# Theta as one product over all 512 columns, a new order of its stage, and two row blocks in each float64 piece

## The chip, the cores and the metric

One core of one Trainium2 chip runs the whole program in one launch. The metric is device time in microseconds of that core. Three runs of the kernel before took 546.91, 547.48 and 551.65 us; their median is 547.48 us.

## The reference

Four batches, 576 tokens. What is computed, in order, all in float32 except where the input is float64:

```python
# 1. attention, 8 heads of 64; heads 0-3 local (32 keys back), 4-7 strided (same position mod 32)
attn = softmax(where(mask, q @ k.T / 8, -1e9)) @ v          # -> x, 4 x 576 x 512
# 2. mixing; its weights arrive as float64
theta = x @ w_theta
y = w_tok_r @ (x * cos(theta)) + w_tok_i @ (x * sin(theta))
u = x + y
x = u + relu(u @ w_ch)
# 3. four experts, two of four taken per token, each a causal attention of 64
out = sum_e gate_e * (softmax(causal(x wq_e (x wk_e).T / 8)) @ (x wv_e) @ wo_e)
```

## The kernel before

Every float32 product that must keep its precision is made of three products of rounded halves (`mm3`, lines 291 to 294): hi by hi, hi by lo, lo by hi. So each operand is split by a copy (hi) and a subtraction (lo).

The **attention** of a batch is worked in four pairs of heads (`attn_pair`), pairs 0 and 1 local, 2 and 3 strided, each in three groups. Its result for batch b goes to the tile `X[b]`, features on the partitions. The attention of batch 0 comes first. That of batch b+1 (`next_pair`) is written between the steps of the mixing of batch b, so that TensorE has something to do in both.

The **mixing** of a batch has five steps. `theta(b, h)` makes, for one half h of the features (256 columns) and five blocks of tokens t (four of 128, one of 64), 12 products of 256 columns, rounds theta/2pi on VectorE (lines 315, 316), and takes the absolute value (line 317), the cosine (line 329) and the sine (line 330) on ScalarE. `rotate(b, h)` transposes x on TensorE into `xn`, multiplies it with cosine and sine (line 348; 354 and 355 for the last block) and splits the result into `z` (lines 358 or 360, and 362). `tokens(b, h)` makes four accumulations `y` of 27 products of 288 columns over the nine row blocks of the token weights `wtk`, adds x (line 377) and splits the sum `u` (lines 386, 387). `channels(b)` makes eight accumulations `g` of 12 products with the weights `wch` and adds them (line 399); it comes one batch later, behind `theta(b+1, 0)`.

The order written out for a batch b over 0 is theta(b,0), pair 0 of b+1, channels(b-1), rotate(b,0), pair 1, theta(b,1), pair 2, rotate(b,1), tokens(b,0), pair 3, tokens(b,1). On ScalarE, sines and exponentials need different tables, and `issue_after` keeps them together: in batches over 0 the ten sines and cosines of a half come behind the last absolute value of that half, and exponentials of pairs 1 and 3 come behind the sines of the half.

The **float64 weights** (`load64`, lines 139 to 145) come by DMA on SyncE's queue, one row block of 128 rows to a piece, into slots of `X[1]` and `X[3]`, four in each. A piece costs one copy on ScalarE (143), one bit operation on VectorE (144), and the split: one activation on ScalarE (106), one subtraction on VectorE (108 or 110). w_theta has 8 pieces of 256 columns, w_tok 18 of 288 in two halves of nine, w_ch 8 of 256.

Buffers that the change touches: `act` (four of the tags ahi and alo) holds the split of x for theta; `zu` (four) holds z of half 0 and then the split u; `z1` holds z of half 1; `rp` (five) holds cosine and sine; in PSUM, `acc` (two banks) holds th, y and g, `s` scores, and in batch 0 also th of odd blocks.

What stands in the program is the wanted order; a planner simulates the engines when the kernel is built and moves instructions of an engine past each other where buffers and `issue_after` allow. The order that runs is its order.

Of the kernel before, what the change touches and what calls it, by code (L numbers as in the profile page):

```python
# [48 lines left out]
def fused_kernel(ctx: ExitStack, tc: tile.TileContext, ql, kl, vl, qs, ks, vs, q0l, q0s, wth, wtk, wch, wqk, wvg, wo, out):  # L49
# [25 lines left out]
    mask_l = new_mask("mask_l", [128, 4, LK], wb)  # L75
# [4 lines left out]
    nc.vector.tensor_copy(mask_l[:64, 2:4, :], mask_l[:64, 1:2, :].to_broadcast([64, 2, LK]))  # L80
# [45 lines left out]
    def load64(dst, src, kt, n0, n1, scale=1.0, late=False):  # L126

        hi, lo = dst
        n = n1 - n0
        for c in range(kt):
            place = X[3] if late or len(pieces) % 2 else X[1]
            raw = place.bitcast(U16)[:, len(pieces) // (1 if late else 2) % 4, :4 * n]
            pieces.append(c)
            st = X[2][:, c % 4, HALF:HALF + n]
            nc.sync.dma_start(raw[:, :4 * n - 1], src[:, c, n0:n1].bitcast(U16)[:, 1:])
            mid = raw.bitcast(U32).rearrange("p (n t) -> p n t", t=2)[:, :, 0]  # L140
# [45 lines left out]
    def attn_pair(b, pair, ps1, apl, deep):  # L186
# [6 lines left out]
        for g, (j0, j1) in enumerate(groups):  # L193
# [4 lines left out]
            mask = mask_l[:, min(g, 1):min(g, 1) + 3, :] if local else mask_s[:, 2 * (g // 2):2 * (g // 2) + n, :]  # L198
# [103 lines left out]
    def theta(b, h):  # L302
        if h == 0:
            xsplit[b] = split_x(b)
        xs = xsplit[b]
        d0 = 256 * h
        for t in range(NT):
            w, t0 = TW[t], 128 * t
            th = ps1.tile([128, 512], F32, tag="s" if b == 0 and t % 2 else "acc", bufs=2, name=f"th_{b}_{h}_{t}")
            for c in range(4):  # L310
                turned = mm3(th[:w, :256], xs[c][0][:, t0:t0 + w], xs[c][1][:, t0:t0 + w],
                             wth_hi[:, c, d0:d0 + 256], wth_lo[:, c, d0:d0 + 256], c == 0, c == 3)
            cs = rp.tile([128, 2, 256], F32, tag="cs", name=f"cs_{b}_{h}_{t}")
            r = cs[:w, 1, :]
            nc.vector.tensor_scalar_add(r, th[:w, :256], MAGIC)
            nc.vector.scalar_tensor_tensor(r, r, MAGIC, th[:w, :256], op0=ALU.subtract, op1=ALU.subtract)  # L316
            last = nc.scalar.activation(cs[:w, 0, :], r, AF.Abs)
            trig[h, t] = cs
            if b == 0:
                sines(b, h, range(t, t + 1))  # L320
# [5 lines left out]
    def sines(b, h, tiles):  # L326
        for t in tiles:
            w, cs = TW[t], trig[h, t]
            nc.scalar.activation(cs[:w, 0, :], cs[:w, 0, :], AF.Sin, bias=halfpi[:w], scale=-TWO_PI)
            sins[b, h] = nc.scalar.activation(cs[:w, 1, :], cs[:w, 1, :], AF.Sin, scale=-TWO_PI).ins  # L330

    def rotate(b, h):
        for t in range(NT):
            w, t0, cs = TW[t], 128 * t, trig[h, t]
# [4 lines left out]
            if t < 4:  # L339
                zf = cs  # L340
                if h == 0:
                    hi = zu.tile([128, S], F32R, tag="zuhi", name=f"zhi_{b}_{h}_{t}")
                    lo = zu.tile([128, S], F32R, tag="zulo", name=f"zlo_{b}_{h}_{t}")
                else:
                    hi = z1.tile([128, 512], F32R, tag=f"zhi{t}", name=f"zhi_{b}_{h}_{t}")
                    lo = z1.tile([128, 512], F32R, tag=f"zlo{t}", name=f"zlo_{b}_{h}_{t}")
                hi, lo = (v[:, :512].rearrange("p (a c) -> p a c", a=2) for v in (hi, lo))
                nc.vector.tensor_tensor(zf, cs, xn[:, None, :256].to_broadcast([128, 2, 256]), op=ALU.mult)
                z[h, t], z[h, 4 + t] = (hi[:, 0, :], lo[:, 0, :]), (hi[:, 1, :], lo[:, 1, :])
            else:  # L350
# [51 lines left out]
    nc.gpsimd.memset(halfpi, math.pi / 2)  # L402
    spark = const.tile([128, 1], F32, name="spark")
# [5 lines left out]
    with tc.tile_pool(name="ps0", bufs=2, space=PSUM) as ps0, tc.tile_pool(name="ain0", bufs=9) as ain0, \  # L409
# [445 lines left out]
```

## Time and profile before

| | |
|---|---|
| median of three runs | 547.48 us |
| the profiled execution | 551.44 us, span 549.6 us |
| TensorE (PE) busy | 524.4 us, 95% |
| VectorE (DVE) busy | 402.3 us, 73% |
| ScalarE (ACT) busy | 319.7 us, 58% |
| GpSimd (POOL) busy | 195.4 us, 36% |
| chain that ended last | PE 72%, DVE 12%, ACT 6%, DMA 6% |

Times count from the start of the span. A busy PE is one that has a product in flight; since products overlap, two that follow each other show their true cost by the distance of their starts. The attention of batch 0 lasts to about 36 us, the mixing with the attention of the other batches to about 346 us, the experts to the end.

### The profile page before, as it was taken

What the parts mean: (1) busy time and instruction counts of PE and PEld (TensorE: products, weight loads), DVE (VectorE), ACT (ScalarE), POOL (GpSimd) and SP (SyncE); (2) the same over time, 40 slices, a digit from 0 to 9 for tenths busy, and PEclk for the clock granted to TensorE, in tenths of its full rate; (3) what the DMA queues carried; (4) which work ended last, traced back from release to release, by engine and by line L of the source; (5) the groups of instructions that cost most, each with busy time, mean ns of one, the idle gap of its engine ahead of it and who ended that gap; (6) DMA issues with size and microseconds to landing.
All of it is one profiled execution on the core that took longest, in us unless ns stands there. A gap on an engine that the chain in (4) does not pass through costs nothing.

```text
span 549.6 us, 12463 instructions
## 1 busy us (share of the span) xinstructions
PE 524.4 (95%) x4500; PEld 499.9 (91%) x4500; DVE 402.3 (73%) x1269; ACT 319.7 (58%) x906; POOL 195.4 (36%) x280
## 2 busy tenths in 40 slices
PE   6798999989999999999999999999999999999997
PEld 5688899989999999989999999979988998999987
DVE  5979996765857576855456443699998888888972
ACT  4988984426362163352145431487788767867873
POOL 5100013320643112642006462175456443625541
PEclk9959999989999999999999999999999999999999
DMA  9967243550202131000100021000001001100112
GB/s 263 282 189 257 82 162 99 172 180 24 68 23 90 35 131 35 24 23 2 58 0 1 2 60 38 1 2 1 1 16 61 14 1 45 44 1 10 36 45 87
DMA packets 20389, 36.63 MB, mean 67 GB/s; under 512 B 2904, under 2 KB 12296, under 8 KB 20328
## 3 DMA queue, kind: packets, MB, share of 16 engines
q1 hardware_dynamic: 20328, 35.83, 20.4%
q8 instruction: 36, 0.59, 0.5%
q14 instruction: 25, 0.20, 0.1%
HBM read 31.10 MB, written 4.72 MB: 65 GB/s over the span
## 4 chain that ended last, share of the span: by engine, by line
PE 72%; DVE 12%; ACT 6%; DMA 6%; issue 2%; POOL 1%; SPq 0%; DVEq 0%; ACTq 0%; POOLq 0%
PE y L292 6%; PE y L293 6%; PE y L294 6%; PE av L269 4%; PE s L205 3%; PE g L292 3%; PE g L294 3%; PE g L293 3%; PE tp L674 3%; PE tp L241 3%; PE th L294 3%; PE th L292 3%; PE th L293 2%; PE pq L292 2%; PE s L633 2%
## 5 line engine op out<-in xcount | busy, mean ns | idle before, releaser
L292 PE MATMUL y<-wtk_hi,zhi 128*128 128x288 f32 x288 | 86.0, 300 | 1.5 <-DVE cs L316 1.1
L293 PE MATMUL y<-wtk_lo,zhi 128*128 128x288 f32 x288 | 85.4, 298 | 0.0
L294 PE MATMUL y<-wtk_hi,zlo 128*128 128x288 f32 x288 | 85.2, 297 | 0.0
L238 POOL TENSOR_TENSOR p<-p,sm 128x288 f32<-128x288 f32 (+2 forms) x36 | 21.9, 615 | 136.8 <-DMA X<-in_wch 58.1
L669 POOL TENSOR_SCALAR p<-p,sm,gt 128x256 f32<-128x256 f32 (+3 forms) x63 | 45.1, 717 | 53.3 <-DVE sm L667 24.9
L292 PEld LDWEIGHTS y<-wtk_hi,zhi 128*128 128x128 f32 x288 | 53.9, 188 | 1.9 <-ACT wtk_hi L106 1.2
L293 PEld LDWEIGHTS y<-wtk_lo,zhi 128*128 128x128 f32 x288 | 54.1, 188 | 0.1
L294 PEld LDWEIGHTS y<-wtk_hi,zlo 128*128 128x128 f32 x288 | 54.0, 188 | 0.0
L362 POOL TENSOR_TENSOR zlo<-cs,zhi 128x512 fp32r<-128x512 f32 (+1 forms) x30 | 36.0, 1214 | 49.0 <-DVE zhi L358 41.3
L292 PE MATMUL th<-wth_hi,x_hi 128*128 128x256 f32 (+1 forms) x160 | 47.6, 299 | 0.9 <-ACT X L276 0.5
L293 PE MATMUL th<-wth_lo,x_hi 128*128 128x256 f32 (+1 forms) x160 | 45.5, 286 | 0.0
L294 PE MATMUL th<-wth_hi,x_lo 128*128 128x256 f32 (+1 forms) x160 | 45.2, 288 | 0.0
L205 PE MATMUL s<-k,q 128*108 128x54 f32 (+2 forms) x320 | 41.3, 270 | 1.1 <-POOL q L175 1.1
L288 POOL TENSOR_TENSOR x_lo<-X,x_hi 128x576 fp32r<-128x576 f32 x20 | 29.4, 1469 | 36.2 <-DVE x_hi L286 30.5
L245 ACT COPY pt<-tp 96x384 f32<-96x384 f32 (+2 forms) x44 | 21.1, 479 | 36.3 <-PE tp L241 35.8
L205 PEld LDWEIGHTS s<-k,q 128*108 128x108 f32 (+1 forms) x320 | 39.4, 192 | 2.0 <-POOL q L175 1.4
L292 PE MATMUL pq<-x_hi,wqk_hi 128*128 128x288 f32 x128 | 39.6, 310 | 1.3 <-DVE q L581 1.1
L292 PE MATMUL g<-u_hi,wch_hi 128*128 128x288 f32 x128 | 38.7, 302 | 0.0
L683 DVE TENSOR_TENSOR ptlo<-tp,pthi 128x128 fp32r<-128x128 f32 (+4 forms) x80 | 37.6, 479 | 1.1 <-ACT pthi L682 0.4
L293 PE MATMUL pq<-x_lo,wqk_hi 128*128 128x288 f32 x128 | 37.9, 296 | 0.0
L293 PE MATMUL g<-u_lo,wch_hi 128*128 128x288 f32 x128 | 37.8, 295 | 0.0
L294 PE MATMUL pq<-x_hi,wqk_lo 128*128 128x288 f32 x128 | 37.8, 295 | 0.0
(183 smaller groups left out, 1713.9 us busy)
## 6 DMA issues: line engine op xcount, KB each, us to landing
X<-in_wtk SPq DMA_DIRECT2D x18, 287.8 KB
q<-in_ql SPq DMA_DIRECT2D x7, 576.0 KB
q<-in_qs SPq DMA_DIRECT2D x6, 594.0 KB
v<-in_vl SPq DMA_DIRECT2D x24, 144.0 KB
out_t<-X SPq DMA_DIRECT2D x20, 128.0 KB
k<-in_kl SPq DMA_DIRECT2D x8, 304.0 KB
k<-in_ks SPq DMA_DIRECT2D x8, 288.0 KB
X<-in_wth SPq DMA_DIRECT2D x8, 255.8 KB
```

The costliest lines, as they stand in the source:

```text
L205: nc.tensor.matmul(s[:rm, i * kw:i * kw + w], qt[:, j0 + i, :], kt[:, k0:k0 + w], start=False, stop=i == n - 1)
L238: (nc.vector if b == 0 else nc.gpsimd).tensor_tensor(tiles(p), tiles(p), each(sm), op=ALU.mult)
L241: turned = nc.tensor.transpose(tp[:kw, i * rm:(i + 1) * rm], p[:rm, i * kw:(i + 1) * kw], ident[:rm, :rm])
L245: copy(pt[:kw, :n * rm], tp[:kw, :n * rm])
L269: last = nc.tensor.matmul(av[64 * h:64 * h + 64, c0:c0 + wi], vg[:w, i, h, :], pt[:w, i, h, :wi], start=True, stop=True)
L288: halved[name] = eng.tensor_tensor(lo, x, f(hi), op=ALU.subtract).ins
L292: nc.tensor.matmul(ps, ahi, bhi, start=first, stop=False)
L293: nc.tensor.matmul(ps, ahi, blo, start=False, stop=False)
L294: return nc.tensor.matmul(ps, alo, bhi, start=False, stop=last)
L362: halved[b, h] = eng.tensor_tensor(lo, zf, f(hi), op=ALU.subtract).ins
L669: eng.tensor_scalar(p[:w, :kn], p[:w, :kn], sm[:w, t:t + 1], gt[:w, t, e:e + 1], op0=ALU.mult, op1=ALU.mult)
L683: nc.vector.tensor_tensor(dst(ptlo), src, f(dst(pthi)), op=ALU.subtract)
```

## The change

Theta is made over both halves at once, in products of 512 columns, and one block of tokens at a time: `theta(b, t)`. Rounding, absolute value, cosine and sine work on 512 columns. For the last block of 64 tokens, cosine and sine share one tile of 128 partitions (absolute value in the upper half, with its own bias), so that one activation makes both. In batch 0, the first half of `wtk` is loaded two row blocks at a time between the blocks of theta, and rotate(0,0) runs one block behind; in the others both rotations come behind the whole of theta. z takes buffers of `act` for one half and of `zu` (now six) for the other; `z1` is gone. A float64 piece holds two row blocks where there are two: 4, 10 and 4 pieces, in two slots of double size for each of `X[1]`, `X[3]` and the scratch `X[2]`.

```diff
     def load64(dst, src, kt, n0, n1, scale=1.0, late=False):
-        for c in range(kt):
+        for c in range(*kt, 2):
+            m = min(2, kt[1] - c)
-            raw = place.bitcast(U16)[:, len(pieces) // (1 if late else 2) % 4, :4 * n]
+            i0 = 2 * (len(pieces) // (1 if late else 2) % 2)
+            raw = place.bitcast(U16)[:, i0:i0 + m, :4 * n]
+            j0 = 2 * (len(pieces) % 2)
-            st = X[2][:, c % 4, HALF:HALF + n]
+            st = X[2][:, j0:j0 + m, HALF:HALF + n]
...
-                with tc.issue_after(sins[b - 1, pair // 2]) if (b > 1 and pair % 2) else nullcontext():
+                with tc.issue_after(sins[b - 1]) if (b > 1 and pair == 1) else nullcontext():
...
+    def theta(b, t):
+        w, t0 = TW[t], 128 * t
+        th = ps1.tile([128, DM], F32, tag="s" if b == 0 and t % 2 else "acc", bufs=2, name=f"th_{b}_{t}")
+        for c in range(4):
+            turned = mm3(th[:w], xs[c][0][:, t0:t0 + w], xs[c][1][:, t0:t0 + w], wth_hi[:, c, :], wth_lo[:, c, :],
+                         c == 0, c == 3)
+        if t < 4:
+            cs = rp.tile([128, 2, DM], F32, tag="cs", name=f"cs_{b}_{t}")
+            first = turn = cs[:, 1, :]
+            size = cs[:, 0, :]
+        else:
+            cs = rp.tile([128, DM], F32, tag="cs4", bufs=1, name=f"cs_{b}_{t}")
+            first, turn, size = cs[0:64], cs[64:128], cs[0:64]
...
+        if b == 0:
+            sines(b, range(t, t + 1))
+        elif t == NT - 1:
             with tc.issue_after(last.ins):
-                sines(b, h, range(NT))
+                sines(b, range(NT))
...
+                sins[b] = nc.scalar.activation(cs, cs, AF.Sin, bias=quarter, scale=-TWO_PI).ins
...
     def rotate
+                pool, tags = (act, ("ahi", "alo")) if (b == 0) == (h == 1) else (zu, ("zuhi", "zulo"))
...
-    zu = ph1.enter_context(tc.tile_pool(name="zu", bufs=4))
-    rp = ph1.enter_context(tc.tile_pool(name="rp", bufs=5))
-    z1 = ph1.enter_context(tc.tile_pool(name="z1", bufs=1))
+    zu = ph1.enter_context(tc.tile_pool(name="zu", bufs=6))
+    rp = ph1.enter_context(tc.tile_pool(name="rp", bufs=4))
...
     for b in range(B):
-        theta(b, 0)
+        for t in range(NT):
+            turned = theta(b, t)
+            if b == 0:
+                with tc.issue_after(valued[0]), tc.issue_after(halved["x0_0_3"]):
+                    load64(wtk_s, wtk, (2 * t, min(2 * t + 2, 9)), 0, HALF)
+                if t > 0:
+                    rotate(b, 0, [t - 1])
         if b > 0:
             next_pair(b, 0)
             channels(b - 1)
+            rotate(b, 0)
+            next_pair(b, 1)
+            next_pair(b, 2)
         else:
-            with tc.issue_after(valued[0]), tc.issue_after(halved["x0_0_3"]):
-                load64(wtk_s, wtk, 9, 0, HALF)
-        rotate(b, 0)
-        if b > 0:
-            next_pair(b, 1)
-        turned = theta(b, 1)
-        if b > 0:
-            next_pair(b, 2)
+            rotate(b, 0, [NT - 1])
         rotate(b, 1)
...
         if b == 0:
-            with tc.issue_after(turned), tc.issue_after(sins[0, 1]):
+            with tc.issue_after(turned), tc.issue_after(sins[0]):
                 next_pair(b, 0)
                 next_pair(b, 1)
```

## Rows read from the trace of the kernel before

**Rows 1.** By stretch: us; PE, PEld, DVE, ACT, POOL busy (instructions); granted clock; DMA.

```profile
26.00:36.00 10.00, 9.31 (x107) 7.02 (x105) 7.19 (x22) 7.75 (x25) 0.00 (x0) 0.50 0.43 137
36.00:50.00 14.00, 13.65 (x101) 13.42 (x102) 13.05 (x33) 11.83 (x30) 0.00 (x0) 0.88 0.99 339
50.00:58.00 8.00, 5.42 (x44) 4.77 (x43) 7.86 (x20) 7.25 (x20) 0.00 (x0) 1.00 0.10 26
58.00:80.00 22.00, 21.14 (x163) 20.70 (x164) 21.94 (x60) 20.15 (x60) 1.93 (x2) 1.00 0.46 150
98.50:122.00 23.50, 21.57 (x287) 19.95 (x286) 17.78 (x54) 8.44 (x25) 8.25 (x10) 0.93 0.51 165
122.00:190.00 68.00, 67.94 (x638) 66.80 (x634) 42.60 (x109) 28.90 (x63) 22.71 (x23) 1.00 0.18 58
```

**Rows 2.** PE by time: start, us, line, operation, count, idle before and releaser.

```profile
54.34 0.41 PE L338 MATMUL xn<-ident,X 128*128 128x128 f32 x2 [1.66 <-DVE cs L355]
58.16 0.37 PE L292 MATMUL y<-wtk_hi,zhi 128*128 128x288 f32 x1 [1.08 <-DVE cs L316]
112.07 1.39 PE L269 MATMUL av<-pt,v 54*64 54x54 f32 x32 [1.59 <-DMA v<-in_vs]
239.77 0.44 PE L241 MATMUL tp<-ident,p 108*54 108x108 f32 x3 [1.09 <-ACT pt L245]
```

**Rows 3.** The chain that ended last around 107 us: start, us, what.

```profile
106.74 6.01 DMA v<-in_vs
```

**Rows 4.** PE by time: products of 256, 288 and 512 columns that follow each other.

```profile
41.02 0.28 PE L294 MATMUL th<-wth_hi,x_lo 128*128 128x256 f32 x1
41.14 0.28 PE L292 MATMUL th<-wth_hi,x_hi 128*128 128x256 f32 x1
...
231.21 0.29 PE L292 MATMUL y<-wtk_hi,zhi 128*128 128x288 f32 x1
231.34 0.30 PE L293 MATMUL y<-wtk_lo,zhi 128*128 128x288 f32 x1
...
387.37 0.39 PE L633 MATMUL s<-k,q 128*128 128x512 f32 x1
387.60 0.39 PE L634 MATMUL s<-klow,q 128*128 128x512 f32 x1
```

**Rows 5.** DVE, 36 to 80 us, by form: count, busy us, mean ns.

```profile
L144 DVE SCALAR_TENSOR_TENSOR X<-X,X 128x288 uint32<-128x288 uint32 x18 | 7.8, 451 | 0.6 <-ACT X L143 0.6
L348 DVE TENSOR_TENSOR cs<-cs,xn 128x512 f32<-128x512 f32 x8 | 5.4, 680 | 0.3 <-ACT cs L330 0.2
L315 DVE TENSOR_SCALAR cs<-th 128x256 f32<-128x256 f32 x8 | 3.3, 419 | 0.0
```

**Rows 6.** DVE and ACT by time: two that follow each other without a wait.

```profile
52.07 0.75 DVE L315 TENSOR_SCALAR cs<-th 128x256 f32<-128x256 f32 x2
56.05 0.72 ACT L317 ACTIVATE cs<-cs 128x256 f32<-128x256 f32 x2
```

**Rows 7.** ACT, 36 to 80 us, by form: count, busy us, mean ns.

```profile
L360 ACT CAST zhi<-cs 128x512 fp32r<-128x512 f32 x8 | 4.9, 614 | 0.0
...
L317 ACT ACTIVATE cs<-cs 128x256 f32<-128x256 f32 x8 | 3.2, 412 | 0.0
```

**Rows 8.** Line 329 alone, its table loads: ns min/median/max, first and last start.

```profile
L329 ACT ACT_TABLE_LOAD  x6: 1283/1283/1283, 44.9 to 276.6; - x6
```

**Rows 9.** ACT by time: the last sine of batch 0, batch 1's first exponential.

```profile
65.43 0.40 ACT L330 ACTIVATE cs<-cs 64x256 f32<-64x256 f32 x1
...
68.42 0.34 ACT L222 ACTIVATE p<-s,mx 128x96 f32<-128x96 f32 x1
```

**Rows 10.** Theta's own work by stretch: us, PE, PEld, DVE, clock, DMA.

```profile
98.50:122.00 23.50, 4.74 (x24) 3.38 (x24) 1.53 (x4) 0.93 0.51 165
138.00:153.00 15.00, 8.26 (x60) 7.31 (x60) 3.76 (x9) 1.00 0.25 82
```

**Rows 11.** ACT by time: the last cast of u in the mixing.

```profile
327.47 0.43 ACT L386 CAST u_hi<-X 128x288 fp32r<-128x288 f32 x1
```

More of the change, by code (lines that the diff above doesn't have):

```diff
@@ L300, in fused_kernel @@
     xsplit, trig, z = {}, {}, {}
-    def theta(b, h):
-        if h == 0:
+    def theta(b, t):
+        if t == 0:
             xsplit[b] = split_x(b)
         xs = xsplit[b]
[L306 to L320, printed above, removed]
-        if b > 0:
+        w, t0 = TW[t], 128 * t
[10 more added lines that the diff above has]
+            first, turn, size = cs[0:64], cs[64:128], cs[0:64]
+        nc.vector.tensor_scalar_add(first, th[:w], MAGIC)
+        nc.vector.scalar_tensor_tensor(turn, first, MAGIC, th[:w], op0=ALU.subtract, op1=ALU.subtract)
+        last = nc.scalar.activation(size, turn, AF.Abs)
+        trig[t] = cs
+        if b == 0:
+            sines(b, range(t, t + 1))
+        elif t == NT - 1:
@@ L322, in theta, with sines @@
             with tc.issue_after(last.ins):
-                sines(b, h, range(NT))
+                sines(b, range(NT))
         return turned.ins
-    def sines(b, h, tiles):
+    def sines(b, tiles):
         for t in tiles:
[L328 to L334, printed above, removed]
+            cs = trig[t]
+            if t < 4:
+                nc.scalar.activation(cs[:, 0, :], cs[:, 0, :], AF.Sin, bias=halfpi, scale=-TWO_PI)
+                sins[b] = nc.scalar.activation(cs[:, 1, :], cs[:, 1, :], AF.Sin, scale=-TWO_PI).ins
+            else:
+                sins[b] = nc.scalar.activation(cs, cs, AF.Sin, bias=quarter, scale=-TWO_PI).ins
@@ L335, in rotate @@
+    def rotate(b, h, tiles=range(NT)):
+        for t in tiles:
+            w, t0, hs = TW[t], 128 * t, slice(256 * h, 256 * h + 256)
             tag, bufs = ("av", 2) if b == 0 and t % 3 else ("xn", 1)
@@ L402, in fused_kernel @@
     nc.gpsimd.memset(halfpi, math.pi / 2)
+    quarter = const.tile([128, 1], F32, name="quarter")
+    nc.gpsimd.memset(quarter, 0.0)
+    nc.gpsimd.memset(quarter[:64], math.pi / 2)
     spark = const.tile([128, 1], F32, name="spark")
@@ L450, in fused_kernel @@
             with tc.issue_after(turns[0, 0]), tc.issue_after(halved[0, 0]):
-                load64(wtk_s, wtk, 9, HALF, S)
+                load64(wtk_s, wtk, (0, 9), HALF, S)
         if b == B - 1:
@@ L472, in fused_kernel @@
         if b == 0:
-            with tc.issue_after(sins[0, 1]):
+            with tc.issue_after(sins[0]):
                 for n0 in range(0, DM, 256):
-                    load64(wch_s, wch, 4, n0, n0 + 256, late=True)
+                    load64(wch_s, wch, (0, 4), n0, n0 + 256, late=True)
             next_pair(b, 2)
```

45 lines of the change are left out of this document (19 added, 26 removed).

## The prediction

> **What bounds the kernel now.** I read busy time by stretch first, then PE's own waits, then the chain of waits, then durations by form. By stretch [rows 1], PE is the bound nearly everywhere behind 36 us: 67.94 us busy of 68 from 122 to 190 us. There a shorter VectorE or ScalarE instruction buys nothing. The exception is the mixing of batch 0: DVE is busy 13.05 of 14, 7.86 of 8 and 21.94 of 22 us from 36 to 80 us, ACT 11.83, 7.25 and 20.15. In that stretch the two set when the first token products y can start, and how early the attention of batch 1 comes. PE is seen to pay for it in two places. Between 50 and 58 us it is busy only 5.42 us, with waits of 1.66 and 1.08 us, both ended by DVE [rows 2]; the second is for a bank of PSUM that the rounding of theta's second half still read. From 98.5 to 122 us it is busy 21.57 of 23.5 us, at a granted clock of 0.93, that is, a part of it at 1.2 GHz [rows 1]; here batch 1's attention is late, and its longest wait is for a tile of v [rows 2], a DMA of 6.01 us on the chain [rows 3], issued when an earlier pair gave a buffer back.
>
> **The change part by part.**
>
> Products. 480 products of 256 columns become 240 of 512. Two of 256 columns start 0.12 us apart, two of 512 columns, in the expert stage, 0.23 us [rows 4]: a pair of 0.24 becomes 0.23. The saving is 192 x 0.01 = 1.9 us in the four full blocks. For the 48 pairs of the block of 64 tokens, whose stationary half is narrower, I take nothing. All of it is on PE, hence on the path: **-1.9 us**, between 0 (0.01 us is a row's last digit) and 240 x 0.01 = -2.4. The Trainium skill, TensorE: Matmul & The Clock Gate, section Back-to-back issue gap, gives a sustained spacing of about 81 ns for 128 and 131 ns for 512 columns; by that rule, an estimate on a straight line puts 256 at 98 ns and the saving at 240 x (196 - 131) ns = 15.6 us. The 0.23 us on record speak against it; it is a rival below.
>
> Rounding, absolute value, cosine, sine in batch 0. On DVE a form of 256 takes 0.419 us, one of 512 that also reads PSUM 0.680 [rows 5], and a pair without a wait 0.75 [rows 6]; a merge saves 0.07 to 0.16 us. On ACT a pair of 256 takes 0.72 us [rows 6], or 2 x 0.412 where they stand apart, and 512 columns 0.614 [rows 7]. A merge saves 0.11 to 0.21, and the last block's four activations become one, some 0.8 us less (2 x 0.72 - 0.61).
>
> Float64 pieces. 18 pieces of w_tok become 10 and 8 of w_ch 4, 12 merges of four instructions each, DVE and ACT two. From 0.451 us at 288 columns and 1.02 ns a column (0.261 us for 256, [rows 5]) a double piece is about 0.745 us, an estimate: the same saving of 0.07 to 0.16. The DMAs move the same bytes in fewer issues on SyncE's queue; a queue that waits for a slot now waits for a double one, and the q, k and v loads of batch 1 stand behind it. DVE saves 10 + 24 = 34 merges, 2.4 to 5.4 us, ACT 5 + 8 + 24 = 37, 4.1 to 7.8, and 0.8 more. That is all between 36 and 98 us. The w_theta pieces are hidden behind PE, which is busy 9.31 of 10 us at half clock from 26 to 36 us [rows 1]: 0, between -1.0 and +0.5 if a longer piece stands before an attention step; were that cover gone, 8 DVE merges would give 0.6 to 1.3 us.
>
> The order in batch 0. Before z of half 0 is whole, DVE must now round both halves: 5 x (2 x 0.680 - 2 x 0.419) = 2.6 us more, and ACT has 4 x 3 x (0.614 - 0.41) = 2.4 us more. Against this stand the merged pieces of w_tok's first half (eight merges, 0.6 to 1.3 on DVE) and that the kernel before rounded part of half 1 in that time as well. So z of half 0 comes about when it came. But PE has all 60 products of theta, 13.8 us, ahead of it, the y products need no bank that rounding holds, and the rotation runs one block behind theta, so that eight of the nine row blocks can be used before the last is ready. Of the 2.6 us that PE idles from 50 to 58 us I take **-1.5**, between -2.6 and +2.0. The upper end is two 1-us delays: the sine table (1.28 us [rows 8]) inside the loop, and a double piece ahead of a rotation.
>
> Attention of batch 1. Its exponentials wait for the last sine, which ended at 65.8 us, and for a table; the first came at 68.42 [rows 9]. The last sine will now follow theta's last block, between 55 and 58 us. The pairs cannot come 8 us earlier, since DVE is full to 80 us, but by what DVE saves, some 4. What is there to win from 98.5 to 122 us is 1.9 us idle and 23.5 x 0.07 = 1.6 us lost to the clock [rows 1]: **-2.5**, between 0 and -3.6. Next late is the v DMA, then DVE's scores. A new wait: z of half 1 takes `act` in batch 0, and the split of x for batch 1 needs these buffers, so it waits for the last y. Theta of batch 1 did not start before 98.5 us either (24 of its products fall there, [rows 10]), so I cost it at 0; covered by attention, up to 1 us if that runs dry.
>
> Batches 1 to 3. One sine table instead of two in batches 1 and 2: of six loads behind line 329 [rows 8] four remain, and two returns to exponentials go, 4 x 1.283 = 5.1 us of ACT. Nearly all of it is off the path; the wait of 1.09 us for an ACT copy [rows 2] sat behind such a block: **-0.5**, between -1.1 and 0. z of half 0 no longer waits for channels to free `zu`, which costs and gives nothing while PE is full.
>
> Two of the four u tiles now wait until the last y has freed a z buffer. Only at the end of batch 3 do channels follow at once. There the cast takes 0.43 us [rows 11], the add before and the subtraction behind it each about the 0.45 us of 288 columns on DVE [rows 5]; the first two row blocks of two accumulations (12 products of 288 columns, about 1.6 us) are cover. **+0.8**, between 0 and +1.8; without cover it is two casts and two subtractions.
>
> Sum: -1.9 - 1.5 - 2.5 - 0.5 + 0.8 = -5.6 us. Against the profiled execution, 551.44 - 5.6 = 545.8. That execution stands 4.0 us above the median of 547.48, so for the median 541.9. The bounds, added, reach from -10.7 to +4.3 us: 537 to 552.
>
> **The rivals.**
>
> Hidden anyway. If PE's gain at 58 us only widens the gap before 122 us, because the v DMA and DVE set the pace, the products and the u wait stay: 547.5 - 1.9 + 0.8 = 546.4. For it: 6.01 us of DMA on the chain [rows 3]. Against: that DMA's buffer comes free by attention that waits for the sines. The same time results if the planner moves theta back between other work, so that the order is hardly new.
>
> Slower: filler lost. In batches 1 and 2 half 1 of theta, 60 products each, ran between attention and rotation (the first of the two, [rows 10]), 60 x 0.12 = 7.2 us apiece. Now they run earlier. It decides where z of half 0 is not whole when channels end. Behind theta's end come 0.6 us of absolute value, 1.28 of table, nine activations of 0.61, then product and split: some 9 us, against 96 x 0.13 = 12.5 us of channels [rows 4]. If ACT's exponentials or DVE take more than these 3.5 us, PE idles. With half the filler lost in each, 7.2 us: 547.5 + 7.2 - 1.9 + 0.8 = 553.6; with all of it 560.8. For it: PE has no idle time to give there. Against: attention pairs 1 and 2 and the second half's transposes are free to move in.
>
> Longer steps. In batch 0 a block's chain is DVE 2 x 0.68, ACT 3 x 0.61, DVE 0.68, ACT 0.61, DVE 0.68, together 5.2 us; DVE's own share with a double piece is 4 x 0.68 + 2 x 0.745 = 4.2. If the engines alternate instead of overlapping, y starts 5 x 1.0 us later than thought, and loses the 1.5: -5.6 + 6.5 = +0.9, so 548.4. The Trainium skill, Perfetto Trace Analysis, section Optimizing Scalar/DVE Operations, says the same as a rule: engines that are not saturated but leave bubbles on others may do better with smaller instructions. By the trace DVE is saturated there, so it bears this case out little.
>
> Cheap wide products. If a product of 512 columns followed the next as closely as one of 288, 0.13 us [rows 4], 240 x 0.11 = 26.4 us would go instead of 1.9: 547.5 - 26.4 - 3.7 = 517.4. The rule cited above for the Trainium skill's sustained spacing would, by the estimate made there, give 528.2. For it: nothing on record; against: the two products of 512 columns shown.
>
> **How the numbers follow.** Forecast 0.55 (own range 537 to 546.5, half of it below 542.0), hidden 0.12, filler lost 0.19, longer steps 0.11, wide products 0.03. One per cent, 5.5 us, is about what a measurement of this kernel can tell from no change: 542.0 and 553.0 are the edges. Faster by more: half of 0.55, and 0.03, with a little for both gains at their ends: 0.32. Slower by more: filler lost and a little of the longer steps, 0.21. Within: 0.47. The range leaves out the wide products and the worse half of the filler case: 536.5 to 555.
>
> **What would show it.** Theta's products of 512 columns 0.23 us apart; y's first product near 56 us and fewer waits on PE before it; batch 1's first exponential near 60 us; the gap before 122 us smaller, with the x split of batch 1 behind the last y; four sine table loads; PE without new idle time between 125 and 240 us. I am wrong if PE waits for z of half 0 in batches 1 to 3, if the first y comes after 60 us, or if the attention of batch 1 ends as late as before.

## The result, and the profile after

The changed kernel takes **552.19 us** (median of 14 runs, 551.40 to 555.05), the kernel before 548.75 us on the same chip (14 runs). The ratio is 1.0062, 95% interval 1.0039 to 1.0084: 3.4 us slower, by less than one per cent. The forecast's likeliest case was 5.6 us the other way. The runs of the kernel before scatter more (546.83 to 552.99 us, and one of 708.47), so that the lowest times of the two, 546.83 and 551.40, lie 4.6 us apart. The profile of after has a span of 550.2 us; PE is busy 523.9 us (95%), DVE 397.8 (72%), ACT 300.6 (55%), POOL 196.4 (36%). DVE and ACT have less to do than before, PE no more, and still it takes longer. The chain that ended last now goes 67% by PE (72% before) and 8% by ACT (6%).

By stretch, after (columns as in [rows 1]):

```profile
36.00:50.00 14.00, 13.71 (x55) 10.96 (x56) 11.44 (x18) 9.18 (x15) 0.00 (x0) 0.86 0.96 338
50.00:58.00 8.00, 7.01 (x46) 5.33 (x45) 6.81 (x12) 7.64 (x15) 0.00 (x0) 1.00 0.06 22
58.00:80.00 22.00, 18.27 (x136) 16.55 (x135) 21.79 (x49) 17.08 (x41) 3.42 (x4) 1.00 0.37 120
98.50:122.00 23.50, 23.50 (x244) 21.40 (x242) 17.08 (x46) 6.72 (x15) 9.49 (x10) 1.00 0.41 128
122.00:190.00 68.00, 66.94 (x614) 62.85 (x614) 44.07 (x108) 24.04 (x47) 23.57 (x25) 1.00 0.17 57
```

From 50 to 58 us PE gained, 5.42 to 7.01 us, as forecast; from 58 to 80 us it lost nearly twice as much, 21.14 to 18.27. DVE and ACT, which set the pace there, now stand idle more of the time from 36 to 50 us: DVE is busy 11.44 us instead of 13.05, ACT 9.18 instead of 11.83. Before 122 us the gap is gone; from 122 to 190 us PE idles 1.06 us, where it idled 0.06.

PE's new waits from 55 to 80 us that are longer than 0.4 us (start, us, operation; idle before and releaser), in place of the first two of [rows 2]:

```profile
56.15 0.40 PE L292 MATMUL y<-wtk_hi,zzulo 128*128 128x288 f32 x1 [0.56 <-DVE zzulo L361]
57.23 0.40 PE L290 MATMUL y<-wtk_hi,zzuhi 128*128 128x288 f32 x1 [0.42 <-DVE cs L317]
60.97 0.40 PE L290 MATMUL y<-wtk_hi,zzuhi 128*128 128x288 f32 x1 [1.02 <-ACT zzuhi L359]
69.56 0.30 PE L199 MATMUL s<-mask_l,twice 128*128 128x288 bf16 x1 [1.26 <-DVE p L225]
71.05 0.37 PE L290 MATMUL y<-wtk_hi,zzuhi 128*128 128x288 f32 x1 [0.55 <-DVE X L376]
76.73 0.41 PE L291 MATMUL y<-wtk_lo,zzuhi 128*128 128x288 f32 x1 [0.53 <-DVE wtk_lo L108]
```

Five of the six sit inside y: it starts at 53.5 us instead of 58.2, and then waits for z, for a bank of PSUM, for the add of an earlier y and for a piece of w_tok. The longest is of batch 1's attention: its scores s wait for DVE.

The rows that answer to [rows 4, 5, 8, 9]. PE's products by time, two that follow each other:

```profile
40.14 0.39 PE L290 MATMUL th<-wth_hi,x_hi 128*128 128x512 f32 x1
40.37 0.39 PE L291 MATMUL th<-wth_lo,x_hi 128*128 128x512 f32 x1
```

DVE by form, 36 to 80 us:

```profile
L142 DVE SCALAR_TENSOR_TENSOR X<-X,X 128x576 uint32<-128x576 uint32 x8 | 6.3, 803 | 0.2
L316 DVE TENSOR_SCALAR cs<-th 128x512 f32<-128x512 f32 x4 | 2.7, 686 | 0.0
```

The table loads of the sine's line, and ACT by time at the first exponential of batch 1:

```profile
L331 ACT ACT_TABLE_LOAD  x4: 1283/1283/1283, 48.3 to 281.9; - x4
```

```profile
60.00 0.34 ACT L220 ACTIVATE p<-s,mx 128x96 f32<-128x96 f32 x1
```

These are as forecast: 0.23 us between products, four table loads, the first exponential at 60 us. The time went elsewhere.

**Where it went.** For each product on PE I take the distance to the next start beyond the median distance of its kind (same output, same shape), and add up the excesses over 0.04 us; waits, queueing and half clock all show in it. Behind 330 us every column has 24.8 to 25.1 us more, which the sums leave out. "Before" is the unchanged kernel run once more (a0); the column beside it is the execution that the prediction read.

| lost between products, us | read | before (a0) | after | c2 | d1 | d3 | e2 |
|---|---|---|---|---|---|---|---|
| 0 to 50 us | 16.3 | 16.2 | 15.7 | 16.6 | 16.5 | 16.2 | 16.1 |
| 50 to 58 | 3.3 | 2.8 | 1.7 | 1.9 | 1.5 | 2.5 | 1.1 |
| 58 to 80 | 1.4 | 1.3 | **5.5** | 3.1 | 5.9 | 2.6 | 2.9 |
| 80 to 100 | 0.9 | 1.0 | 1.8 | 1.3 | 1.4 | 1.3 | 1.0 |
| 100 to 130 | **6.3** | 3.4 | 1.8 | 2.1 | 1.9 | 2.2 | 3.2 |
| 130 to 160 | 1.2 | 1.5 | 2.4 | 2.4 | 2.4 | 2.4 | 1.5 |
| 160 to 300 | 7.6 | 7.4 | 6.8 | 6.9 | 6.9 | 7.0 | 7.3 |
| 300 to 330 | 1.0 | 0.9 | **4.2** | 3.3 | 1.7 | 1.5 | 0.9 |
| sum | 38.1 | 34.4 | 39.8 | 37.6 | 38.2 | 35.8 | 34.1 |
| span | 549.6 | 545.5 | 550.2 | 548.6 | 548.2 | 546.1 | 544.9 |

After against a0: 5.4 us more are lost between products, 0.7 less is spent on the rest (550.2 - 39.8 against 545.5 - 34.4), together the 4.7 us between the two spans. Two stretches carry it: batch 0 from 58 to 80 us, +4.2, and the tail of batch 3, +3.3. The two columns of the kernel before also show that of the 6.3 us lost from 100 to 130 us in the execution that was read, 2.9 were this one execution's own.

### The profile page after: what moved, and what is told of

Its sections match the earlier page's. It is cut to its first block, busy times and chain, and to the rows that moved or that the text cites. A ratio compares the mean times of both kernels' runs of the same rounds, so it can differ in the third digit from the quotient of the medians.

```text
span 550.2 us, 11729 instructions
## 1 busy us (share of the span) xinstructions
PE 523.9 (95%) x4260; PEld 483.3 (88%) x4260; DVE 397.8 (72%) x1197; ACT 300.6 (55%) x806; POOL 196.4 (36%) x282
## 4 chain that ended last, share of the span: by engine, by line
PE 67%; DVE 13%; ACT 8%; DMA 5%; issue 3%; POOL 2%; SPq 0%; POOLq 0%; DVEq 0%; ACTq 0%
PE y L291 5%; PE y L292 5%; PE y L290 5%; PE av L267 4%; PE tp L677 3%; PE s L203 3%; PE tp L239 3%; PE th L290 3%; PE th L292 3%; PE th L291 2%; PE g L290 2%; PE pq L290 2%; PE g L291 2%; PE g L292 2%; PE s L636 2%
## 5 line engine op out<-in xcount | busy, mean ns | idle before, releaser
L672 POOL TENSOR_SCALAR p<-p,sm,gt 128x256 f32<-128x256 f32 (+3 forms) x63 | 44.9, 715 | 53.5 <-DVE sm L670 25.0
L361 POOL TENSOR_TENSOR zalo<-cs,zahi 128x512 fp32r<-128x512 f32 x12 | 15.6, 1301 | 73.9 <-DVE zahi L357 60.1
L290 PE MATMUL y<-wtk_hi,zzuhi 128*128 128x288 f32 x128 | 38.5, 302 | 3.3 <-DVE X L376 1.8
L292 PE MATMUL y<-wtk_hi,zzulo 128*128 128x288 f32 x128 | 38.0, 298 | 1.6 <-POOL zzulo L361 1.0
L291 PE MATMUL y<-wtk_lo,zzuhi 128*128 128x288 f32 x128 | 38.3, 300 | 0.6 <-DVE wtk_lo L108 0.5
L290 PE MATMUL y<-wtk_hi,zahi 128*128 128x288 f32 x128 | 38.8, 303 | 0.0
L292 PE MATMUL y<-wtk_hi,zalo 128*128 128x288 f32 x128 | 38.3, 302 | 0.0
L291 PE MATMUL y<-wtk_lo,zahi 128*128 128x288 f32 x128 | 37.9, 297 | 0.0
L292 PE MATMUL g<-u_hi,wch_lo 128*128 128x288 f32 x128 | 37.7, 294 | 0.0
L677 PE MATMUL tp<-ident,p 128*128 128x128 f32 (+1 forms) x240 | 36.4, 265 | 0.6 <-DVE ptlo L686 0.6
L685 ACT CAST pthi<-tp 128x128 fp32r<-128x128 f32 (+4 forms) x80 | 32.9, 426 | 7.5 <-PE tp L677 6.5
```

The costliest lines, as they stand in the source:

```text
L290: nc.tensor.matmul(ps, ahi, bhi, start=first, stop=False)
L291: nc.tensor.matmul(ps, ahi, blo, start=False, stop=False)
L292: return nc.tensor.matmul(ps, alo, bhi, start=False, stop=last)
L672: eng.tensor_scalar(p[:w, :kn], p[:w, :kn], sm[:w, t:t + 1], gt[:w, t, e:e + 1], op0=ALU.mult, op1=ALU.mult)
L677: nc.tensor.transpose(tp[:, c * w:(c + 1) * w], p[:w, 128 * c:128 * c + 128], ident[:w, :w])
L685: nc.scalar.copy(dst(pthi), src)
```

## The experiments

Each ratio is to the kernel before on the same chip, with its 95% interval. In the diffs, "..." stands for lines left out. The changed kernel stands at 1.0062; 0.001 is 0.55 us.

**a0, a1, a2: the kernel before again, and the pieces.** a0 changes nothing. a1 is the kernel before with the pieces of two row blocks alone; a2 is the changed kernel with pieces of one row block:

```diff
-        for c in range(*kt, 2):
-            m = min(2, kt[1] - c)
+        for c in range(*kt):
...
```

Expected, a0: 

> The kernel before, unchanged, for a second profile of it. Theory (the execution profiled before was a slow one of its kind: 551.44 us against a median of 548.75): a ratio of 1.00, and a span of 545 to 546 us, in which the half clock from 114.5 to 117.9 us and most of the 5.9 us that TensorE lost between 100 and 120 us are missing; what is gained there in the changed kernel's profile was then never there to gain. Rival (the waits between 100 and 120 us are the kernel's own): they stand in this profile too, within 1 us.

Expected, a1: 

> The kernel before with the float64 pieces of two row blocks alone. Theory (the new order and the shared buffers cost the time, the pieces are a small gain): ratio to the kernel before 0.996 to 1.001. Rival (longer pieces stall VectorE, ScalarE and SyncE's queue in the first 80 us): 1.004 to 1.010, with the first y product after 59 us.

Expected, a2: 

> The changed kernel with its pieces of one row block again. Theory (order and buffers cost it): 551.5 to 554 us, ratio 1.005 to 1.010. Rival (the pieces cost it): 546 to 549 us, ratio 0.997 to 1.001.

Measured: a0 548.30 us, 0.9988 (0.9951 to 1.0025). a1 547.98, 0.9977 (0.9946 to 1.0009). a2 551.30, 1.0033 (0.9999 to 1.0068). The pieces are not the loss: a1 is level with before. a2 alone would not decide it, since its interval reaches from no loss to the whole of it, but it loses 6.1 us from 58 to 80 us where the changed kernel loses 5.5. a0's span of 545.5 us is as its theory had it. Its stretches in batch 0 and before 122 us:

```profile
50.00:58.00 8.00, 5.91 (x48) 5.28 (x47) 7.91 (x21) 7.25 (x21) 0.00 (x0) 1.00 0.15 42
58.00:80.00 22.00, 21.30 (x167) 20.82 (x166) 21.94 (x60) 20.13 (x62) 1.93 (x2) 1.00 0.42 138
98.50:122.00 23.50, 23.02 (x313) 21.29 (x313) 18.57 (x54) 8.96 (x26) 8.23 (x10) 1.00 0.58 189
```

PE idles 0.48 us before 122 us at full clock, where [rows 1] had 1.93 us at 0.93; the wait of 1.59 us for a tile of v [rows 2] is not there.

**b1, b4: the order in batch 0.** b1 keeps products of 512 but puts all of theta first, then w_tok's first half in one go, then the rotation. b4 holds back w_tok's pieces behind the rounding of earlier blocks.

```diff
 b1
-            if b == 0:
...
-                    load64(wtk_s, wtk, (2 * t, min(2 * t + 2, 9)), 0, HALF)
-                if t > 0:
-                    rotate(b, 0, [t - 1])
+        if b == 0:
...
+                load64(wtk_s, wtk, (0, 9), 0, HALF)
+            rotate(b, 0, range(NT - 1))
 b4
+                done = (rounded[t - 2], sized[t - 2]) if t > 1 else (halved["x0_0_3"], valued[0])
-                with tc.issue_after(valued[0]), tc.issue_after(halved["x0_0_3"]):
+                with tc.issue_after(done[0]), tc.issue_after(done[1]):
```

Expected, b1: 

> The changed kernel with batch 0 in the order of before: all of theta, then the first half of w_tok, then rotate(0,0). Theory (in batch 0 the wide blocks and the pieces between them leave VectorE and ScalarE without work from 42 to 50 us, whatever is written first, since the planner orders them): 551 to 554 us, ratio to the kernel before 1.005 to 1.011. Rival (the interleaved order of batch 0 is the loss): 547.5 to 550 us, ratio 0.999 to 1.004.

Expected, b4: 

> The changed kernel with the third to fifth piece of w_tok's first half, in batch 0, behind the rounding and the absolute value of theta's blocks 0 to 2. Theory (the first rounding stands in VectorE's queue behind a piece whose DMA lands at 43.0 us, so ScalarE's first sine comes at 49.6 us): the first sine at 45.5 to 47 us, the last y of batch 0 two to three us earlier, 549 to 550.5 us, ratio 1.001 to 1.004. Rival (the y products then wait for these pieces, and nothing is won): 551.5 to 553 us.

Measured: b1 551.53 us, 1.0061 (1.0038 to 1.0084), no change. b4 554.37, 1.0115 (1.0090 to 1.0140), 2.9 us worse than the changed kernel, outside both of its cases: DVE then had little to do (8.47 us busy of 14 from 36 to 50 us). Its first rounding waits for PE, in b4; in the changed kernel, whose lines come second here, two steps of w_tok's pieces stand right before it on DVE:

```profile
44.62 1.33 DVE L317 TENSOR_SCALAR cs<-th 128x512 f32<-128x512 f32 x2 [2.90 <-PE th L292]
```

```profile
43.59 0.46 DVE L142 SCALAR_TENSOR_TENSOR X<-X,X 128x288 uint32<-128x288 uint32 x1 [0.85 <-ACT X L141]
44.13 0.76 DVE L108 TENSOR_TENSOR wtk_lo<-X,wtk_hi 128x576 fp32r<-128x576 f32 x1
44.81 0.69 DVE L316 TENSOR_SCALAR cs<-th 128x512 f32<-128x512 f32 x1
```

Theta's first product starts at 37.64 us in b4 and at 36.29 after, so against it the rounding came 1.5 us sooner without the pieces (6.98 us behind it, 8.52 after, 5.59 in a0). The rest is theta's first block itself.

**b2: two products of 256 for each of 512**, everything else as changed.

```diff
+        for d in (slice(0, 256), slice(256, DM)):
+            for c in range(4):
+                turned = mm3(th[:w, d], ..., wth_hi[:, c, d], wth_lo[:, c, d], c == 0, c == 3)
```

Expected: 

> The changed kernel with theta's products of 256 columns again, two for one, into the same tile. Theory (a product of 512 costs two of 256 less 0.01 us): 1 to 2.5 us more than the changed kernel, 553 to 555 us, ratio 1.008 to 1.013. Rival (wide products are cheap): 560 us or more. Rival (nothing at all): 551.5 to 552.5 us.

Measured: 552.59 us, 1.0079 (1.0052 to 1.0106). The wide products save some 0.9 us by this, less than the 1.9 forecast, and the intervals overlap, so that the saving isn't clear of the noise. In b2 two products of 256 start 0.118 us apart (median), 0.007 more a pair than one of 512.

**c2: batch 0 in halves.** The changed kernel, but batch 0 makes theta for half 0 (products of 256), loads w_tok, rotates half 0, and only then makes theta for half 1. The z buffers and batches 1 to 3 stay as changed.

```diff
+            for t in range(NT):
+                theta(b, t, slice(0, 256))
...
+                load64(wtk_s, wtk, (0, 9), 0, HALF)
+            rotate(b, 0)
+            for t in range(NT):
+                turned = theta(b, t, slice(256, DM))
```

Expected: 

> The changed kernel with batch 0 in the order and the widths of the kernel before: theta of 256 columns for all five blocks, then w_tok's first half, the rotation of half 0, theta of the other half, the rotation of half 1. Batches 1 to 3 keep products of 512 and the new order; z keeps its new buffers. Theory (about half of the 4.5 us that lie between the two kernels arises in batch 0, where both halves must be rounded before y can start): y starts at 53 to 55 us, TensorE's excess between 50 and 80 us falls from 7.2 towards 4.1 us, and the time falls by 1.5 to 3 us, to 549 to 550.5. Rival 1 (the loss there comes with the buffers or with the attention of batch 1, not with theta's order): the time stays within 0.7 us of the changed kernel. Rival 2 (what batch 0 wins is lost in the attention of batch 1): y starts early, the end of y of batch 0 is early, and the span is as before.

Measured: 550.28 us, 1.0025 (1.0004 to 1.0045): **2.0 us come back**, by the theory; but y starts at 59.4 us, not at 53 to 55. An early start of y was not what counts. b1 has this order of theta, w_tok and rotation at full width and gains nothing, so it is the halves that do it; c2 makes the steps narrower and lets z of half 0 wait for half 0 alone, and these two aren't told apart. On DVE, the first rounding and the last subtraction of z of half 0, in a0, after and c2 in this order:

```profile
40.97 0.42 DVE L315 TENSOR_SCALAR cs<-th 128x256 f32<-128x256 f32 x1
...
54.78 0.42 DVE L362 TENSOR_TENSOR zlo<-cs,zhi 128x256 fp32r<-128x256 f32 x1
```

```profile
44.81 0.69 DVE L316 TENSOR_SCALAR cs<-th 128x512 f32<-128x512 f32 x1
...
62.83 0.41 DVE L361 TENSOR_TENSOR z8lo<-cs,z8hi 128x256 fp32r<-128x256 f32 x1
```

```profile
42.62 0.42 DVE L319 TENSOR_SCALAR cs<-th 128x256 f32<-128x256 f32 x1 [0.48 <-issue]
...
57.91 0.42 DVE L363 TENSOR_TENSOR z8lo<-cs,z8hi 128x256 fp32r<-128x256 f32 x1
```

z of half 0 is whole at 55.2 us in a0, at **63.2 after**, and at 58.3 in c2. Between them lies the chain of the first block, at the double width and with engines that wait for each other (ACT, then DVE, after):

```profile
47.14 1.18 ACT L318 ACTIVATE cs<-cs 128x512 f32<-128x512 f32 x2 [2.61 <-DVE cs L317]
48.34 1.28 ACT L331 ACT_TABLE_LOAD   x1
```

```profile
50.91 0.69 DVE L348 TENSOR_TENSOR cs<-cs,xn 128x512 f32<-128x512 f32 x1 [1.93 <-ACT cs L332]
```

**c4: batch 1's attention later.** Its first two pairs are released by z of half 1 instead of the last sine.

```diff
-            with tc.issue_after(turned), tc.issue_after(sins[0]):
+            with tc.issue_after(turns[b, 1]), tc.issue_after(halved[b, 1]):
                 next_pair(b, 0)
```

Expected: 

> The changed kernel with the first two pairs of batch 1's attention released by the split of z of half 1 in batch 0 rather than by the last sine. Theory (the attention that now comes 8 us earlier takes VectorE and ScalarE from the rotation, and y waits): batch 1's first exponential comes at 66 to 70 us as in the kernel before, the waits of TensorE between 58 and 75 us fall from 4.7 to under 2.5 us, y of batch 0 ends before 100 us, and the time falls by 1 to 2 us, to 550 to 551. Rival (the early attention is what is won in batch 0, and y waits for the rounding of both halves anyway): y ends earlier, but batch 1's attention is late, and the time is the same or up to 3 us longer, 552 to 555.

Measured: 553.19 us, 1.0074 (1.0047 to 1.0101), the rival by its time. The exponential came at 68.53 us, but PE waited 3.6 us for DVE's add, and its granted clock fell to half (PE by time, then by stretch):

```profile
69.12 0.58 PE L290 MATMUL y<-wtk_hi,zzuhi 128*128 128x288 f32 x1 [3.63 <-DVE X L376]
```

```profile
67.50:74.30 6.80, 5.18 (x22) 5.21 (x22) 6.80 (x16) 5.31 (x14) 0.43 (x1) 0.50 0.26 79
```

Early or late, that attention hardly matters for the stretch from 100 to 130 us: 2.2 us lost here, 2.1 in c2 with its first exponential at 67.44, 1.8 after.

**d2, e2: two subtractions on POOL.** zlo of row blocks 1 and 3 of half 0 in batch 0 go from DVE to POOL, which is idle there: d2 on the changed kernel, e2 on the kernel before.

```diff
-            eng = nc.gpsimd if b > 0 else nc.vector
+            eng = nc.gpsimd if b > 0 or h == 0 and t % 2 else nc.vector
```

Expected, d2: 

> The changed kernel with the subtractions zlo of row blocks 1 and 3 of half 0 of batch 0 on GpSimd, idle there, instead of VectorE. Theory A (VectorE's load in 50 to 66 us makes y wait): 1.4 us of VectorE go, y's waits of 2.1 us between 58 and 66 us fall by half, and the time falls by 0.5 to 1.5 us. Theory B (y waits for the length of the chain round, absolute value, cosine, sine, product, split, each step twice as wide and ended by the next): a subtraction on GpSimd takes 1.6 us instead of 0.63, the chain gets longer, and the time is the same or up to 1.5 us longer.

Expected, e2: 

> The kernel before with that last edit alone: the subtractions zlo of row blocks 1 and 3 of half 0 of batch 0 on GpSimd. Theory (there z of half 0 is whole at 55 us and VectorE is full to 80 us, so 0.7 us less work on it is worth something): 0 to 1 us faster, 547.2 to 548.2. Rival (the chain is longer and y starts later): 548.2 to 549.5.

Measured: d2 551.08 us, 1.0043 (1.0021 to 1.0065), which lies in theory A's range, some 1 us; but its interval holds the changed kernel's 1.0062. Of the 2.0 us lost from 58 to 66 us 1.0 remain, and from 58 to 80 us 5.1 of 5.5. A subtraction took 1.3 us on POOL, not the 1.6 of theory B. e2 **546.88, 0.9963 (0.9938 to 0.9987)**, 2.0 us under the kernel before and more than expected: the lowest median of all versions. By stretch, e2:

```profile
50.00:58.00 8.00, 7.19 (x60) 6.86 (x59) 7.45 (x20) 7.66 (x22) 2.46 (x2) 1.00 0.02 6
58.00:80.00 22.00, 20.63 (x156) 19.38 (x155) 21.94 (x61) 19.19 (x60) 1.79 (x2) 1.00 0.46 151
```

PE's idle time from 50 to 58 us falls from 2.09 us (a0) to 0.81 with two subtractions of 1.3 us on POOL. But from 58 to 80 us e2 loses 2.9 us where a0 loses 1.3 (table above), and their spans differ by 0.6 us, as the lowest times of e2 and of the kernel before beside it do by 0.7 (546.11 and 546.80). Where the 2.0 us between the medians come from isn't shown.

**a3, b3, c1, d1: the tail of batch 3.** In the waits of PE from 298 to 330 us of after (total, times, longest) stand

```profile
PE y L290 <- DVE X L376: 1.3, 1, 1.3
PE y L292 <- POOL zzulo L361: 1.0, 1, 1.0
```

and on POOL, then DVE, of the same kernel stand

```profile
308.49 3.35 POOL L286 TENSOR_TENSOR x_lo<-X,x_hi 128x576 fp32r<-128x576 f32 x2 [0.56 <-ACT x_hi L282]
311.80 1.32 POOL L361 TENSOR_TENSOR zzulo<-cs,zzuhi 128x512 fp32r<-128x512 f32 x1
313.08 2.75 POOL L108 TENSOR_TENSOR wqk_lo<-wqk_st,wqk_hi 128x512 fp32r<-128x512 f32 x2
```

```profile
313.56 4.96 DVE L386 TENSOR_TENSOR u_lo<-X,u_hi 128x288 fp32r<-128x288 f32 x4 [1.57 <-ACT u_hi L385]
```

where a0 has

```profile
292.58 3.34 POOL L288 TENSOR_TENSOR x_lo<-X,x_hi 128x576 fp32r<-128x576 f32 x2 [2.33 <-ACT x_hi L284]
...
308.40 1.28 POOL L362 TENSOR_TENSOR zlo<-cs,zhi 128x512 fp32r<-128x512 f32 x1 [2.61 <-ACT zhi L360]
```

```profile
305.83 1.20 DVE L387 TENSOR_TENSOR u_lo<-X,u_hi 128x288 fp32r<-128x288 f32 x3 [1.41 <-ACT u_hi L386]
```

z of half 0 now lies in `act`, so the split of x for the experts cannot start before the last y of half 0 has read it. It moved from 292 to 308 us, into the rotation of half 1, and stands in POOL's queue ahead of the zlo that y waits for. u comes later, and its first four subtractions take 1.24 us each beside POOL's wqk_lo, where three in a0, with POOL idle, take 0.40; the add of the next y stands behind them. Four edits (a3's second line, for the weights, and b3's aren't shown): a3 puts both the split of x and the weights behind z; b3 the split alone behind the last cast of u; c1 the weights alone behind the first casts of u; d1 both c1's edit and the split of x behind z.

```diff
 a3, d1
+    with tc.issue_after(halved[B - 1, 1]):
+        xsplit[0] = split_x(0)
 c1, d1: the weights' block stands behind tokens(b, 0), in it
-                with tc.issue_after(turns[b, 1]):
+                with tc.issue_after(us['last']):
                     wqk_hi, wqk_lo = load_split(wc, ws, wqk, 4, 512, "wqk")
```

Expected, a3: 

> The changed kernel, with the split of x for the experts and the split of their weights put behind the last z of batch 3 on GpSimd. Theory (in batch 3 the last blocks of z stand behind this work on GpSimd, since z and u share buffers; TensorE waits 1.03 and 1.29 us for it at 312 and 318 us): 2 to 2.5 us less than the changed kernel, ratio to the kernel before 1.001 to 1.003, no wait of TensorE on GpSimd near 312 us. Rival (these waits are made up later anyway): no change, 1.005 to 1.008.

Expected, b3: 

> The changed kernel with the split of x for the experts behind the last cast of u in batch 3, where GpSimd has room. Theory (the buffers that z and the split of x share move the split from 291 to 307 us, where it meets the last z and the split of the experts' weights on GpSimd, and VectorE's four u subtractions there take 4.96 us, 1.24 each, for 0.46 alone; TensorE waits 1.03 and 1.29 us for that): 1.0 to 2.5 us less than the changed kernel, 549.5 to 551 us, ratio 1.002 to 1.005. Rival (the weights alone fill GpSimd, as in the run that put z first): no gain, 552 us or more.

Expected, c1: 

> The changed kernel, with the loading and splitting of the experts' weights (and the exponential table and masks that stand with it) put behind the first casts of u in batch 3. Theory (in batch 3's tail the four subtractions of u_lo run beside GpSimd's wqk_lo and take 1.24 us each instead of 0.46, and the add of the next y, and with it a PSUM bank, waits for them): they take about 0.5 us each, the wait of 1.29 us of TensorE at 318.9 us goes, and the time falls by 1 to 2.5 us, to 549.5 to 551. Rival 1 (the tail is set by the z of half 1, rotated late behind the x split): the wait of 1.03 us for GpSimd's zlo stays, u_lo gets faster, and the time moves by less than 0.7 us. Rival 2 (the weights come later and the experts wait for them): 552.5 to 554.

Expected, d1: 

> The changed kernel with both of the experts' loads out of the tail's way: the weights behind the first casts of u of batch 3, and the split of x for the experts behind the last subtraction of z. Theory (two things in the tail, the u_lo beside wqk_lo and z behind x_lo on GpSimd; each edit alone left or worsened the other): the wait of 1.2 us for GpSimd's zlo goes too, TensorE's excess between 300 and 330 us falls from 4.2 to under 2 us, and the time falls by 1.5 to 2.5 us against the changed kernel, to 549.5 to 550.7. Rival (z is late by its rotation, behind a DVE that the adds of y fill, whatever GpSimd does first): the wait moves to another line, the excess stays over 3 us, and the time is 551 to 552.

Measured: a3 554.30 us, 1.0089 (1.0058 to 1.0120), above both of its cases; b3 553.84, 1.0098 (1.0073 to 1.0123), its rival, with PE waiting 3.0 us for DVE's add. c1 551.72, 1.0054 (1.0030 to 1.0079), its first rival. d1 **549.54, 1.0006 (0.9981 to 1.0031): 3.1 us come back**. In a3 zlo is in time, but wqk_lo still meets u_lo, and PE waits 3.18 us for DVE's add, and its granted clock is half for most of what follows (DVE by time, then the stretch):

```profile
313.22 5.54 DVE L386 TENSOR_TENSOR u_lo<-X,u_hi 128x288 fp32r<-128x288 f32 x4 [1.25 <-ACT u_hi L385]
```

```profile
318.00:325.50 7.50, 6.31 (x28) 6.32 (x29) 1.50 (x3) 0.60 (x2) 4.56 (x5) 0.54 0.19 55
```

In c1 u_lo is freed but zlo still waits behind x_lo (wait 1.2 us). Only with both does the tail close, from 4.2 to 1.7 us lost between 300 and 330 us; d1's waits from 298 to 330 us are

```profile
PE g L291 <- DVE u_lo L386: 0.5, 1, 0.5
PE y L290 <- DVE X L376: 0.2, 1, 0.2
```

**c3, d3, e1: together.** c3 is c1 and c2; d3 is d1 and c2; e1 is d3 and the subtractions on POOL. No edit is new.

Expected, c3: 

> Both edits together: batch 0 in halves and the experts' weights behind the first casts of u of batch 3. Theory (the two losses are separate and make up the whole difference): the savings add, 546.5 to 548.5, level with the kernel before or just under it, as 192 of the 240 wide products and two table loads fewer are left. Rival (they are not separate, or they aren't the losses): 549.5 to 552.

Expected, d3: 

> Batch 0 in halves, the experts' weights behind the first casts of u of batch 3, and the split of x for the experts behind z. Theory (the losses add up and are all there is): 0.8 to 1.5 us less than with the first two alone, 547 to 548.5, that is 0 to 1 us under the kernel before, about what the products of 512 columns and the two table loads save. Rival: as with the first two alone, 549 to 550, or worse.

Expected, e1: 

> Batch 0 in halves, the experts' weights behind the first casts of u, the split of x behind z, and the subtractions zlo of row blocks 1 and 3 of half 0 of batch 0 on GpSimd. Theory (the gains add, though in halves y waits less for z): 0.3 to 1.2 us less than without the last edit, 547 to 548, ratio 0.997 to 0.9985 to the kernel before. Rival (in halves the subtractions were covered, and on GpSimd a block's chain is a microsecond longer): 548 to 549.5.

Measured: c3 549.63 us, 1.0011 (0.9989 to 1.0033), at the rival's edge; d3 548.35, 0.9988 (0.9966 to 1.0011); e1 547.88, 0.9977 (0.9946 to 1.0009). The two repairs give 2.0 and 3.1 us alone and 4.1 us together; with them the change is level with the kernel before. d3 and e1 lie in the ranges of their theories, but e1's interval holds d3's ratio, and e1 is no faster than e2, which has nothing of the change.

## Why the prediction was wrong

**Products, -1.9.** The distances are as read: 0.229 us against twice 0.120 as medians behind 125 us. In the time b2 makes it some 0.9 us, and what is left of the span without the lost time fell by 0.7. Right in kind, about half the size, and not clear of the noise; two decimals do not carry 0.01 us. The same 0.229 us ends the rival "Cheap wide products".

**Pieces, 0.** Right (a1); a merged piece takes 0.803 us on DVE where 0.745 was estimated.

**The order in batch 0, -1.5.** This is the step that failed: "So z of half 0 comes about when it came." The working set DVE's and ACT's added busy time (2.6 and 2.4 us) against savings, as if both stayed full. They did not: z of half 0 came 8.0 us later (55.2 in a0, 63.2 after). The first rounding is 3.8 us later (40.97 to 44.81 us): theta begins 0.9 us later (35.38 to 36.29), its first block covers both halves, and steps of w_tok's pieces stand before the rounding. Then every step of the block's chain is wider, and little else is ready for the engines meanwhile: DVE and ACT do 1.6 and 2.7 us less than in [rows 1] from 36 to 50 us. Of the forecast gain, 1.1 us came before 58 us; 4.2 us from 58 to 80 us and 0.8 behind them pay for it, so the term of -1.5 measures +3.9.

Only 1.02 us of the new waits from 58 to 80 us is for z itself; the others, 1.26, 0.55 and 0.53 us, are for work on DVE, which is busy 21.79 of 22 us there. That the late z pushed this work together is argued; c2, with z 4.9 us sooner, loses 3.1 us in that stretch instead of 5.5.

The rival "Longer steps" had this mechanism and priced it at +0.9 in all; it held the chance of 0.11 because DVE was seen full. From 40 to 50 us DVE is busy 9.54 us in a0, 9.13 in c2 and 7.92 after: what the prediction saw as full was full with steps of half the width. The Trainium skill, Perfetto Trace Analysis, section Optimizing Scalar/DVE Operations, cited there, advises smaller instructions where engines that are not saturated cause bubbles on others; c2 agrees, 2.0 us.

**Attention of batch 1, -2.5.** The loss from 100 to 130 us did fall, by 1.6 us against a0, but not for the reason given: c2 and c4 have the attention as late as before and keep the gain. And a1, whose order is the old one, loses only 2.4 us there, so that perhaps 0.6 of the 1.6 us is the new order's. Another 2.9 us of what was read [rows 1 to 3] belonged to one execution, with its half clock and its late tile of v. The prediction noted that this execution stood 4.0 us above the median, and still took terms from that stretch and subtracted them from the median. What brings the gain was not tried; all of theta of batch 1 now lies from 108 to 132 us as work for PE.

One of the prediction's signs of being wrong came true here, "the attention of batch 1 ends as late as before". It began 8.4 us sooner than in the execution read (60.00 to 68.42 us), and its last copy into X starts later than in that execution, shown first, and in a0, where it starts at 112.39 us; the last line is of after:

```profile
115.19 0.41 DVE L276 COPY X<-av 128x144 f32<-128x144 f32 x1 [0.54 <-PE av L269]
```

```profile
117.72 0.40 DVE L274 COPY X<-av 128x144 f32<-128x144 f32 x1
```

PE is full there (23.50 of 23.50 us), so that this costs nothing by itself.

**Batches 1 to 3, -0.5.** The gain is there: 7.4 to 6.8 us lost from 160 to 300 us, and the wait of 1.09 us of [rows 2], which a0 has too, is gone after. But from 130 to 160 us 0.9 us more are lost, in two waits of after that a0 doesn't have:

```profile
144.64 0.40 PE L290 MATMUL g<-u_hi,wch_hi 128*128 128x288 f32 x1 [0.46 <-DVE X L398]
...
147.14 0.53 PE L239 MATMUL tp<-ident,p 128*96 128x128 f32 x3 [0.41 <-POOL p L236]
```

PE thus has new idle time between 125 and 240 us, against the forecast, but the two nearly cancel. "Filler lost", which put 7.2 us there, did not happen.

**u tiles, +0.8.** The second step that failed. Right place, wrong cause, a quarter of the size: +3.3 us. The prediction followed `act` in batch 0 and found its new wait harmless; it did not follow the same buffer in batch 3, where the next to ask for it is the experts' split, and POOL's and DVE's queues behind it were not read. d1, which takes both out of z's and u's way, shows it: 2.5 of the 3.3 us in that stretch, 3.1 in the time.

The sum as measured, by stretch: -0.7 for the rest, -0.5 to 50 us, -1.1, +4.2 and +0.8 in batch 0, -1.6, +0.9, -0.6, +3.3 in the tail: +4.7 us between two spans, +3.4 by the timed runs.

## What to carry to other kernels

Merging instructions pays on an engine that has other work ready; in a chain of engines that hand one block on, it makes the first result later, so follow when the first operand is whole, not how much busy time is saved. When a buffer changes its owner, ask in every stage, the last too, who takes it next and what stands behind that on each queue. And before a gap in one profile becomes a term of the sum, look whether a second execution has it.

## What the runs showed of the hardware

A subtraction of 128x288 on DVE with both operands in SBUF took 0.40 us each with POOL idle (1.20 for three, a0), and 1.24 to 1.39 us (4.96 and 5.54 for four, after and a3) while POOL ran subtractions back to back (2.75 us for two of wqk_lo, after). The Trainium skill, SBUF — State Buffer, section Who interferes with whom, says that a DVE instruction with two SBUF inputs contends with a GpSimd instruction that reads SBUF, and that the port pair which they share is an exclusive lock. The rows agree, each u_lo lasting about one of POOL's subtractions (1.38 us for a wqk_lo).

Beside the two longest waits of PE, 3.63 us in c4 and 3.18 us in a3, lie stretches of 6.8 and 7.5 us at a granted clock of 0.50 and 0.54, that is wholly or mostly at 1.2 GHz: there a wait of PE cost more than its own length.
